# A linear-attention and gated-MLP kernel on one core: chunks 10 to 13 in the paired token layout, SBUF products on GpSimd alone from chunk 4 on, and another written-out order

## The chip, the core and the metric

The kernel runs on one of the eight cores of a Trainium2 chip. The core has a matrix engine (TensorE, PE in the profile), a vector engine (VectorE, DVE), an activation engine (ScalarE, ACT), a programmable engine (GpSimd, POOL) and a queue engine (SyncE, SP), which here does nothing but issue DMAs. Every engine takes its instructions strictly in the order in which they were written for it; between engines semaphores keep the order of data. The metric is the device time of one execution in microseconds (us). Three runs of the kernel before took 197.98, 200.19 and 202.25 us, median 200.19 us.

## The reference

There are 4 batches, 8 heads, 768 tokens and 48 numbers per head. The attention keeps a 48 x 48 state per head that is decayed and added to at each token; its output (3072 tokens by 384) goes through a two-layer MLP whose gate is `h * cos(h)`:

```python
f = 1.0 / (1.0 + np.exp(-f_logit))
for t in range(S):
    state = f[:, :, t, :, None] * state + np.einsum('bhd,bhe->bhde', k[:, :, t], v[:, :, t])
    y[:, :, t] = np.einsum('bhd,bhde->bhe', q[:, :, t], state)
# x = y as 3072 x 384
h = x @ w_in              # 384 -> 2048
out = (h * np.cos(h)) @ w_out   # 2048 -> 384
```

## The kernel before

**Tiling.** The 3072 tokens are 24 chunks of 128 tokens. Two chunks make a pair `n` (0 to 11), and three pairs a batch. Attention works pair by pair; the MLP works in units of `m`: units 0 and 1 are the two chunks of pair 0, and unit `m` from 2 on is pair `m - 1`.

**Attention of a pair**, by the names of its steps (`n.u` is the pair and which half of it; the uncut steps have no half):

- `f`, `k`, `q`, `v`: loads from HBM, issued on SP.
- `ex`, `ln` (ACT): log of the forget gate; `cum` (PE): running sums within a chunk; `eb`, `ei` (ACT): the decays `b` and `bi`.
- `qm` and `km`: the products q times b and k times bi, both factors in SBUF, result in bf16 in tile `qk`. `vb`: the cast of v to bf16. These may run on GpSimd or VectorE (`vb` on ScalarE too).
- `tq` (and `tk`): the transpose of the products into `qkt`. For pairs 0 to 3 it is done by PE into PSUM and copied out (`qkt`); for pairs 4 to 11 it is one DMA transpose per half, issued on SP.
- `sc` (PE): scores; `am` (DVE): mask, PSUM to SBUF. `ps` (PE), `st` (DVE) and `sz` (two instructions, r = 0 and 1): the new state and its decay. `sz` from tile `st` has both factors in SBUF and may run on GpSimd or VectorE.
- `y` and `yi` (PE): the output, from the scores and from the old state. `yb` (ACT or DVE): its cast. `tx`: its transpose into `x`, for pairs 4 to 10 one DMA transpose per half on SP, otherwise PE and a copy `xe`.

**MLP of a unit**: `h` (PE, eight steps), `co` (ACT, cosine), `g` (DVE, h times cosine, from PSUM and SBUF), `o` (PE, four steps per chunk), `ot` (copy) and `out` (store, on SP). `w` loads the weights and `wc` casts them.

**Two layouts.** In the paired layout (function `pair`) a partition holds two consecutive tokens, so that a run in HBM is 384 bytes; the even and odd tokens are separate blocks on PE. In the other (function `orderly`) a partition holds one token, a run is 192 bytes, and each of `f`, `k`, `q`, `v` is two DMAs per pair instead of one. Which pairs are orderly is set by `ORDERLY`, in the kernel before pairs 5 to 11, which are chunks 10 to 23. `gate` writes `g` straight for orderly pairs (L673) and swaps even and odd tokens back for the others (L677).

**Order.** The text `ORDER` sets everything. A word such as `km4.1:V2` says: step `km4.1` next, on the engine of that letter (T PE, S ACT, V DVE, G POOL, Y SP), and with which buffer. Function `emit` walks the words and issues each step, so an engine's order is that of its words. There is no scheduler behind it. `zf` steps are matmuls on zeros, whose results nobody reads.

Names that differ only in a number are buffers of a small pool: `qk` has 3 buffers, `x` 4, `yb` 4, `g` 5; the four PSUM tiles of 1024 columns are shared by all.

Of the kernel before, what the change touches and what calls it, by code (L numbers as in the profile page):

```python
# [183 lines left out]
def describe(nc, cpool, ppool, q, k, v, f_logit, moe_w_in, moe_w_out, out):  # L184
    G = Graph()
# [5 lines left out]
    def copy(e, o, i):  # L191
        (nc.scalar.copy if e == "ACT" else eng(e).tensor_copy)(out=o, in_=i)  # L192
# [629 lines left out]
```

## Time and profile before

| what | value |
|---|---|
| three runs | 197.98, 200.19, 202.25 us |
| profiled execution, its own time | 198.68 us |
| its span, first to last instruction | 196.9 us |
| busy: PE, DVE, ACT, POOL | 171.2, 145.2, 124.8, 58.1 us |
| mean granted TensorE clock | 0.991 |
| DMA queue q1 | 109024 packets, 35.47 MB, 79.4% of 16 engines' span |

The profile is one execution. Busy times are summed per engine; PE's overlapping matmuls make its share look fuller than it is. A row of the waits reads "who waited, for whom: us in total, times, longest". A row of the timeline reads "start, duration, engine, line, operation, result and operands, count", with the idle time of the engine ahead of it and what ended that in brackets. The rows of one tile give the shortest, median and longest duration in ns. SPq is the queue of DMA issues on SP.

### The profile page before, as it was taken

The page shows a single profiled execution, that of the slowest core. Times are in us where ns is not written, and L with a number is a line of the kernel's source. Part 1 is how long each engine was busy: PE and PEld are TensorE (multiplying, and loading weights), DVE is VectorE, ACT ScalarE, POOL GpSimd, SP SyncE. Part 2 cuts the span into 40 slices and gives each one's busy share as a digit, 9 for nine tenths or more (in the row PEclk, how much of TensorE's full clock was granted, in tenths as well). Part 3 has the DMA queues.
Part 4 walks back from the last instruction along what each step waited for, and adds up shares of the span by engine and source line. Part 5 has one row for each costly group of instructions (what it writes and reads, how often), then busy time and mean ns, then how long its engine had stood idle before and what let it go on. Part 6 is the DMA issues. An engine that isn't in the chain of part 4 may idle for free.

```text
span 196.9 us, 4992 instructions
## 1 busy us (share of the span) xinstructions
PE 171.2 (87%) x2077; PEld 126.2 (64%) x2077; DVE 145.2 (74%) x196; ACT 124.8 (63%) x149; POOL 58.1 (30%) x72
## 2 busy tenths in 40 slices
PE   7438879997999799798787998897989999999993
PEld 3227659966768556586576855674658866778651
DVE  6087988988799997588737894497689998667431
ACT  4936987996778767577456869596458730257401
POOL 3092489657009113511030201650251242000000
PEclk9997999999999999999999999999999999999999
DMA  6999999999995788798977999799949926402013
GB/s 148 272 262 309 379 290 320 228 338 265 188 251 127 83 172 174 179 199 156 210 142 152 226 192 180 165 172 223 198 108 188 191 46 139 150 3 83 0 40 122
DMA packets 109047, 35.79 MB, mean 182 GB/s; under 512 B 102368, under 2 KB 107488, under 8 KB 109024
## 3 DMA queue, kind: packets, MB, share of 16 engines
q1 hardware_dynamic: 109024, 35.47, 79.4%
q8 instruction: 16, 0.26, 0.6%
q14 instruction: 7, 0.06, 0.1%
HBM read 25.17 MB, written 4.72 MB: 152 GB/s over the span
## 4 chain that ended last, share of the span: by engine, by line
PE 48%; DMA 13%; DVE 6%; SPq 4%; ACT 2%; issue 2%; POOL 1%; DVEq 0%; POOLq 0%; ACTq 0%
PE ps L695 22%; PE ps L711 19%; DMA x<-yb 5%; DMA v<-in_v_dram 4%; DMA qkt<-qk 4%; DVE am L416 2%; SPq L385 2%; SPq L311 1%; PE ps L413 1%; PE ps L464 1%; DVE g L677 1%; PE ps L581 1%; PE ps L426 1%; PE ps L458 1%; DVE st L437 1%
## 5 line engine op out<-in xcount | busy, mean ns | idle before, releaser
L695 PE MATMUL ps<-x,w_in_bf 128*128 128x256 bf16 (+1 forms) x624 | 67.1, 264 | 9.6 <-DMA x<-yb 6.3
L711 PE MATMUL ps<-w_out_bf,g 128*128 128x384 bf16 x384 | 71.3, 326 | 0.0
L700 ACT ACTIVATE co<-ps,halfpi 128x1024 bf16<-128x1024 f32 x48 | 52.6, 1113 | 27.0 <-PE ps L695 26.8
L695 PEld LDWEIGHTS <-w_in_bf 128*128 128x128 bf16 x624 | 56.2, 98 | 18.4 <-issue 7.2
L711 PEld LDWEIGHTS <-g 128*128 128x128 bf16 x384 | 34.8, 98 | 19.3
L673 DVE TENSOR_TENSOR g<-ps,co 128x1024 bf16<-128x1024 f32 x28 | 33.6, 1220 | 9.2 <-ACT co L700 8.6
L677 DVE TENSOR_TENSOR g<-ps,co 128x1024 bf16<-128x1024 f32 x20 | 25.2, 1308 | 3.8 <-ACT co L700 2.7
L372 POOL TENSOR_TENSOR qk<-k,bi 128x384 bf16<-128x384 f32 x9 | 9.5, 1064 | 32.8 <-ACT bi L362 16.8
L416 DVE TENSOR_TENSOR am<-ps,upper 128x1024 bf16<-128x1024 f32 x14 | 16.7, 1220 | 2.5 <-PE ps L413 2.2
L192 ACT COPY ot<-ps 128x384 f32<-128x384 f32 x12 | 5.6, 479 | 12.2 <-PE ps L711 12.2
L192 DVE COPY ot<-ps 128x384 f32<-128x384 f32 x12 | 6.6, 551 | 9.1 <-PE ps L711 9.1
L533 POOL TENSOR_TENSOR qk<-q,b 128x384 bf16<-128x384 f32 x7 | 7.4, 1061 | 17.2 <-ACT b L524 10.0
L585 DVE TENSOR_TENSOR am<-ps,pmask 128x1024 bf16<-128x1024 f32 x10 | 12.0, 1215 | 0.6 <-PE ps L581 0.6
L372 POOL TENSOR_TENSOR qk<-q,b 128x384 bf16<-128x384 f32 x8 | 8.3, 1047 | 13.0 <-ACT b L362 11.2
L192 ACT CAST yb<-ps 128x384 bf16<-128x384 f32 x11 | 5.3, 479 | 10.4 <-PE ps L458 8.8
L533 DVE TENSOR_TENSOR qk<-k,bi 128x384 bf16<-128x384 f32 x5 | 7.6, 1539 | 4.9 <-ACT bi L520 4.8
L192 POOL CAST vb<-v 128x768 bf16<-128x768 f32 x7 | 6.4, 915 | 15.2 <-DMA v<-in_v_dram 15.2
L626 POOL TENSOR_TENSOR sz<-st,b 64x192 bf16<-64x192 f32 x9 | 4.8, 528 | 18.5 <-DVE st L619 18.3
L750 ACT ACT_TABLE_LOAD x7 | 9.0, 1283 | 0.8 <-PEq L806 0.7
L192 DVE CAST yb<-ps 128x384 bf16<-128x384 f32 x13 | 7.0, 548 | 3.3 <-PE ps L464 1.8
L700 ACT ACT_TABLE_LOAD x7 | 9.0, 1283 | 0.5 <-DVE x L192 0.4
L362 ACT ACTIVATE bi<-ps 128x768 f32<-128x768 f32 x7 | 5.7, 812 | 4.5 <-PE ps L356 4.1
(87 smaller groups left out, 210.9 us busy)
## 6 DMA issues: line engine op xcount, KB each, us to landing
out_dram<-ot SPq DMA_DIRECT2D x24, 192.0 KB, 2.2
f<-in_f_logit_dram SPq DMA_DIRECT2D x18, 192.0 KB, 3.5
q<-in_q_dram SPq DMA_DIRECT2D x18, 192.0 KB, 4.1
k<-in_k_dram SPq DMA_DIRECT2D x18, 192.0 KB, 4.3
g<-in_moe_w_in_dram SPq DMA_DIRECT2D x4, 768.0 KB, 8.5
g<-in_moe_w_out_dram SPq DMA_DIRECT2D x4, 768.0 KB, 7.6
v<-in_v_dram SPq DMA_DIRECT2D x14, 192.0 KB, 3.5
v<-in_v_dram SPq DMA_DIRECT2D x5, 384.0 KB, 6.1
```

Of the source, the lines that this page charges most:

```text
L192: (nc.scalar.copy if e == "ACT" else eng(e).tensor_copy)(out=o, in_=i)
L362: G.step(f"{nm}{n}", ("ACT",), lambda e, dst=dst, sc=sc, w=w: nc.scalar.activation(out=dst.ap, in_=pc.ap.rearrange("p (g n) -> p g n", g=2 ...
L372: G.step(f"{nm}{n}.{g}", ("POOL", "DVE"), lambda e, g=g, j=j, src=src, dec=dec: eng(e).tensor_mul(out=qkp[g][j].ap[:, :, 0:D], in0=src.ap, ...
L416: G.step(f"am{n}.{g}", ("DVE",), lambda e, g=g, sc=sc: nc.vector.tensor_mul(out=am[g].ap.rearrange("p r b n -> p (r b) n"), in0=sc.ap.rear ...
L533: G.step(f"{nm}{n}.{u}", ("POOL", "DVE"), lambda e, u=u, j=j, src=src, dec=dec: eng(e).tensor_mul(out=qkp[u][j].ap[:, :, :, 0:D], in0=swap ...
L585: G.step(f"am{n}.{u}", ("DVE",), lambda e, u=u, sc=sc: nc.vector.tensor_mul(out=am[u].ap.rearrange("p r b n -> p (r b n)").rearrange("p (y ...
L673: nc.vector.tensor_mul(out=gv.ap, in0=ph.ap.rearrange("p (f n) -> p f n", n=T), in1=co.ap.rearrange("p (f n) -> p f n", n=T))
L677: nc.vector.tensor_mul(out=o.rearrange("p b (n e) -> p b e n", e=2), in0=ph.ap.rearrange("p (b e n) -> p b e n", e=2, n=64), in1=co.ap.rea ...
L695: nc.tensor.matmul(ph.ap[:, i * T:(i + 1) * T].rearrange("p (g t) -> p g t", t=C), lhsT=w_in_bf[:, kk, f0:f0 + 128], rhs=xa[:, :, kk, :], ...
L700: G.step(f"co{m}.{j}", ("ACT",), lambda e, ph=ph, co=co: nc.scalar.activation(out=co.ap, in_=ph.ap, func=AF.Sin, bias=halfpi), reads=[ph], ...
L711: nc.tensor.matmul(po.ap[:, 0:DM], lhsT=gT.ap[:, j, i * C:(i + 1) * C], rhs=w_out_bf[:, j, :], start=(po.first and j == 4 * s), stop=(po.f ...
L750: nc.scalar.preload_act_table_set("natural_log_exp_and_others")
```

## The change

Five things are edited, and `ORDER` is replaced as a whole:

1. `ORDERLY` is pairs 7 to 11 instead of 5 to 11: chunks 10 to 13 go to the paired layout, one DMA per pair and tensor, and their gate to the swapping form.
2. From pair 2 on (chunk 4), `qm`, `km` and the `sz` that read `st` may run on GpSimd alone, `vb` on GpSimd or ScalarE.
3. The casts of weights (`wc`) may run on GpSimd or ScalarE.
4. One matmul on zeros less (`ZEROS`, 14 instead of 15).
5. The new `ORDER` names other engines and another succession for nearly all steps. By engine it has `km` and `qm` 44 times on POOL and 4 times on DVE (before 29 and 19), `sz` 30 times on POOL and 10 on DVE (before 16 and 24), `vb` 7 times on POOL and 5 on ACT (before 7 POOL, 3 DVE, 2 ACT). SP issues 136 DMAs instead of 144; DVE executes 146 steps instead of 177.

```diff
-ORDERLY = range(5, 12)
+ORDERLY = range(7, 12)
-ZEROS = 15
+ZEROS = 14
 ORDER = """
-zf0:T0 zf1:T1 zf2:T2 zf3:T3 zf4:T4 zf5:T5 zf6:T6 zf7:T7 zqk.2:V zsp.1:G zf8:T6 f0.0:Y0 f1.0:Y1
...
+zf0:T0 zf1:T1 zf2:T2 zf3:T3 zf4:T4 zf5:T5 zf6:T6 zf7:T7 zsz.3:V zf8:T6 zsp.0:G f1.1:Y0 ex1.1:S
...
-        G.step(f"wc{part}.{i}", ("POOL", "DVE", "ACT"), lambda e: copy(e, dst.ap, view()),
+        G.step(f"wc{part}.{i}", ("POOL", "ACT"), lambda e: copy(e, dst.ap, view()),
...
-                G.step(f"{nm}{n}.{u}", ("POOL", "DVE"), lambda e, u=u, j=j, src=src, dec=dec: eng(e).tensor_mul(
+                G.step(f"{nm}{n}.{u}", ("POOL", "DVE") if cut else ("POOL",), lambda e, u=u, j=j, src=src, dec=dec: eng(e).tensor_mul(
...
-            G.step(f"vb{n}{u}", ("POOL", "DVE", "ACT"), lambda e, s=s, t=t: copy(e, flat(t.ap), flat(s.ap)),
+            G.step(f"vb{n}{u}", ("POOL", "DVE", "ACT") if cut else ("POOL", "ACT"), lambda e, s=s, t=t: copy(e, flat(t.ap), flat(s.ap)),
...
-                src, ap, who = st, (lambda st=st: st.ap), ("POOL", "DVE")
+                src, ap, who = st, (lambda st=st: st.ap), ("POOL", "DVE") if cut else ("POOL",)
```

The same edits stand in `orderly`, without the `if cut`, since no orderly pair is cut (pairs 0 and 1 are the cut ones: their loads come in halves).

Three places show the new order. The first is DVE and GpSimd around the products of pairs 4 and 5. `qk_2` holds the products of pair 4; its rows are the four of L533 (before) or L532 (after). `am` rows are masks, `g` gates, `x` copies of the transposed output of pair 3. DVE before:

```order
L192 COPY x_3_147<-ps_2_165 128x384
L192 COPY x_3_147<-ps_1_164 128x384
L192 COPY ot_2_159<-ps_2_165 128x384
L533 TENSOR_TENSOR qk_2_121<-k_2_103,bi_2_118 128x8x48 x2
L677 TENSOR_TENSOR g_4_152<-ps_3_166,co_3_156 128x8x2x64
L677 TENSOR_TENSOR g_0_148<-ps_0_163,co_0_153 128x8x2x64
L677 TENSOR_TENSOR g_0_148<-ps_2_165,co_1_154 128x8x2x64
```

DVE after, at the same place (one copy of `x` has gone to ACT):

```order
L191 CAST yb_3_143<-ps_2_165 128x384
L191 COPY x_3_147<-ps_3_166 128x384
L618 TENSOR_TENSOR st_0_138<-ps_0_163,sz_2_136 128x384
L676 TENSOR_TENSOR g_2_150<-ps_1_164,co_3_156 128x8x2x64
L676 TENSOR_TENSOR g_3_151<-ps_2_165,co_0_153 128x8x2x64
L676 TENSOR_TENSOR g_3_151<-ps_0_163,co_1_154 128x8x2x64
L676 TENSOR_TENSOR g_3_151<-ps_3_166,co_2_155 128x8x2x64
```

GpSimd after, the eight products of pairs 4 (`qk_2`) and 5 (`qk_0`) in one file:

```order
L191 CAST vb_1_123<-v_1_108 128x768
L532 TENSOR_TENSOR qk_2_121<-q_2_106,b_2_115 128x8x48
L532 TENSOR_TENSOR qk_2_121<-k_1_102,bi_2_118 128x8x48
L532 TENSOR_TENSOR qk_2_121<-q_2_106,b_2_115 128x8x48
L532 TENSOR_TENSOR qk_2_121<-k_1_102,bi_2_118 128x8x48
L532 TENSOR_TENSOR qk_0_119<-q_1_105,b_0_113 128x8x48
L532 TENSOR_TENSOR qk_0_119<-k_2_103,bi_1_117 128x8x48
L625 TENSOR_TENSOR sz_3_137<-st_0_138,b_1_114 64x4x48
L532 TENSOR_TENSOR qk_0_119<-k_2_103,bi_1_117 128x8x48
```

The two products that stood between the copies and the first gate on DVE stand on GpSimd now, in one row with six others.

The second place is SP around the output transposes of pair 4 (`x_1`), before:

```order
L335 DMA q_1_105<-in_q_dram 128x8x48 x2
L311 DMA_TRANSPOSE x_1_145<-yb_0_140 128x3x128
L718 DMA out_0_dram<-ot_3_160 128x384
L311 DMA_TRANSPOSE x_1_145<-yb_1_141 128x3x128
L335 DMA v_2_109<-in_v_dram 128x8x48
```

and after:

```order
L334 DMA q_0_104<-in_q_dram 128x8x48
L310 DMA_TRANSPOSE x_1_145<-yb_1_141 128x3x128
L310 DMA_TRANSPOSE x_1_145<-yb_0_140 128x3x128
L717 DMA out_0_dram<-ot_3_160 128x384
L290 DMA q_2_106<-in_q_dram 128x8x96
```

The store that stood between the two transposes stands behind them.

The third is SP around the output transposes of pair 5 (`x_0`), before:

```order
L718 DMA out_0_dram<-ot_1_158 128x384
L311 DMA_TRANSPOSE x_0_144<-yb_3_143 128x3x128
L335 DMA q_1_105<-in_q_dram 128x8x48
L335 DMA k_2_103<-in_k_dram 128x8x48
L311 DMA_TRANSPOSE x_0_144<-yb_2_142 128x3x128
```

and after, with the output transposes of pair 6 (`x_2`) at the end:

```order
L310 DMA_TRANSPOSE x_0_144<-yb_3_143 128x3x128
L310 DMA_TRANSPOSE x_0_144<-yb_2_142 128x3x128
L717 DMA out_0_dram<-ot_1_158 128x384
L334 DMA k_2_103<-in_k_dram 128x8x48
L334 DMA q_0_104<-in_q_dram 128x8x48
L334 DMA k_0_101<-in_k_dram 128x8x48
L334 DMA q_1_105<-in_q_dram 128x8x48
L310 DMA_TRANSPOSE x_2_146<-yb_1_141 128x3x128
L310 DMA_TRANSPOSE x_2_146<-yb_0_140 128x3x128
```

The two loads between the transposes of pair 5 have moved, and the transposes of pair 6 stand together behind four loads.

More of the change, by code (lines that the diff above doesn't have):

```diff
@@ new lines @@
+o13.1:T o13.0:T ot13:S2 tq9.0:Y1 sc8.0:T4 am8.0:V1 qm8.1:G f10.0:Y v9.0:Y o11.3:T1 km8.1:G
+cum11.0:T2 tq8.1:Y3 g8.3:V km9.1:G o15.2:T0 tq9.1:Y2 cum11.1:T ei11:S2 sz7.10:G ps8.0:T4 q11.1:Y
+y8.0:T5 o11.0:T eb11:S2 qm11.0:G0 yi8.0:T ex10:S ln10:S0 st8.0:V1 sz8.01:G1 sz8.00:G o11.1:T
+yb8.0:V1 tx8.0:Y1 sc8.1:T6 sc9.0:T2 sc9.1:T4 am8.1:V2 q10.0:Y2 o15.0:T o15.1:T y8.1:T6 yi8.1:T
+yb8.1:S0 out10:Y o11.2:T am9.1:V3 cum10.1:T4 v10.1:Y1 tx8.1:Y vb9:S0 cum10.0:T out5:Y eb10:S1
+o14.3:T7 am9.0:V0 ps9.0:T6 qm10.0:G1 sz9.01:V0 sz9.00:V k11.0:Y2 y9.0:T2 ps9.1:T3 out13:Y ei10:S0
@@ new lines @@
+co10.2:S3 sz9.11:G o16.0:T o12.1:T sc11.0:T2 sc10.0:T4 g10.2:V o17.2:T0 ps10.0:T1 am11.0:V1
+am10.0:V2 st10.0:V1 tq11.1:Y3 o12.2:T o16.3:T ot16:S0 v11.0:Y vb11:S1 sz10.00:G2 sz10.01:G ot12:S3
+sc10.1:T2 sc11.1:T4 am10.1:V0 yi10.0:T1 o17.1:T o19.0:T7 ps10.1:T2 yi10.1:T3 am11.1:V3 y10.1:T
+y10.0:T yb10.1:V1 yb10.0:V0 o18.2:T6 o19.3:T o18.0:T tx10.1:Y2 ps11.0:T3 o17.0:T o17.3:T y11.0:T1
+ot17:S2 y11.1:T4 tx10.0:Y o18.3:T st10.1:V0 sz10.11:G1 sz10.10:G yi11.0:T st11.0:V1 h11.31:T2
+sz11.01:G0 sz11.00:G h11.30:T yb11.0:V3 co11.3:S1 out12:Y yi11.1:T yb11.1:V2 o18.1:T h11.00:T0
@@ new lines @@
+tx11.1:T5 xe11.1:S3 tx11.0:T4 ot18:V3 o19.1:T xe11.0:V h12.30:T4 h12.31:T co12.3:S2 h11.01:T o19.2:T
+g11.3:V4 co11.0:S0 out16:Y h12.10:T2 h12.11:T co12.1:S3 out17:Y ot19:S0 out19:Y g12.3:V3 g11.0:V
+h11.20:T4 h11.21:T h11.10:T0 g12.1:V h12.20:T6 o20.3:T2 co11.2:S1 g11.2:V o21.0:T3 h11.11:T
+co11.1:S2 o22.1:T4 o21.2:T out18:Y g11.1:V o20.0:T o20.2:T h12.01:T0 h12.00:T co12.0:S0 o23.1:T5
+o22.3:T h12.21:T o23.3:T co12.2:S3 g12.0:V o22.0:T o23.0:T g12.2:V out15:Y o21.3:T o22.2:T ot22:S2
+o23.2:T out22:Y ot23:S0 out23:Y o21.1:T ot21:S3 out21:Y o20.1:T ot20:S1 out20:Y
@@ L371, in orderly @@
             for j, (nm, src, dec) in enumerate((("qm", qh[g], bt), ("km", kh[g], bi))):
-                G.step(f"{nm}{n}.{g}", ("POOL", "DVE"), lambda e, g=g, j=j, src=src, dec=dec: eng(e).tensor_mul(
+                G.step(f"{nm}{n}.{g}", ("POOL",), lambda e, g=g, j=j, src=src, dec=dec: eng(e).tensor_mul(
                     out=qkp[g][j].ap[:, :, 0:D], in0=src.ap,
@@ L376, in orderly @@
         vb = Val(vbS)
-        G.step(f"vb{n}", ("POOL", "DVE", "ACT"), lambda e: copy(e, flat(vb.ap), flat(vv.ap)),
+        G.step(f"vb{n}", ("POOL", "ACT"), lambda e: copy(e, flat(vb.ap), flat(vv.ap)),
                reads=[vv], writes=[vb])
@@ L438, in orderly @@
                     out=st.ap, in0=view(), in1=S0.ap), reads=[ps[g], S0], writes=[st])
-                src, ap, who = st, (lambda st=st: st.ap), ("POOL", "DVE")
+                src, ap, who = st, (lambda st=st: st.ap), ("POOL",)
             for r in range(2):
@@ L620, in pair @@
                     out=st.ap, in0=view(), in1=S0.ap), reads=[ps[g], S0], writes=[st])
-                src, ap, who = st, (lambda st=st: st.ap), ("POOL", "DVE")
+                src, ap, who = st, (lambda st=st: st.ap), ("POOL", "DVE") if cut else ("POOL",)
             for r in range(2):
```

129 lines of the change are left out of this document (55 added, 74 removed).

## The prediction

> **What bounds the kernel now.** I read the page first, then busy times by stage, then PE's waits, then the timeline at the longest of these. The page's first row and one stage (columns from the third on: PE, PE weight loads, DVE, ACT, POOL busy us, granted clock, DMA share, GB/s):
>
> ```profile
> PE 171.2 (87%) x2077; PEld 126.2 (64%) x2077; DVE 145.2 (74%) x196; ACT 124.8 (63%) x149; POOL 58.1 (30%) x72
> 26.70:47.10 20.40, 18.53 (x294) 15.70 (x294) 18.50 (x21) 17.10 (x18) 14.07 (x15) 1.00 1.06 289
> ```
>
> PE is the bound, but not a full one: 196.9 less 171.2 leaves it idle for 25.7 us. DVE is next, and in the stage shown it is busy for as long as PE. GpSimd has 70% of its time free. So time is to be had where PE stands still, and PE's waits say for whom (total us, times, longest):
>
> ```profile
> PE ps L695 <- DMA x<-yb: 6.3, 5, 1.8
> PE ps L561 <- DVE qk L533: 2.6, 2, 1.7
> PE ps L413 <- DMA qkt<-qk: 1.7, 3, 1.0
> PE ps L695 <- DVE g L677: 1.2, 1, 1.2
> PE ps L695 <- DVE x L192: 1.1, 1, 1.1
> ```
>
> The largest is the MLP's first layer waiting for the DMA transpose of the attention output. The two waits for DVE in L695 have one story. The timeline around them, DVE, POOL and PE:
>
> ```profile
> 44.73 1.80 DVE L533 TENSOR_TENSOR qk<-k,bi 128x384 bf16<-128x384 f32 x1
> 44.65 1.47 POOL L192 CAST w_out_bf<-g 128x1536 bf16<-128x1536 f32 x1 [0.65 <-DMA g<-in_moe_w_out_dram]
> 47.11 0.38 PE L695 MATMUL ps<-x,w_in_bf 128*128 128x256 bf16 x2 [1.14 <-DVE x L192]
> 61.51 3.91 DVE L533 TENSOR_TENSOR qk<-k,bi 128x384 bf16<-128x384 f32 x2
> 60.86 0.99 POOL L372 TENSOR_TENSOR qk<-k,bi 128x384 bf16<-128x384 f32 x1
> 63.55 0.99 POOL L372 TENSOR_TENSOR qk<-q,b 128x384 bf16<-128x384 f32 x1
> 65.35 2.47 DVE L677 TENSOR_TENSOR g<-ps,co 128x1024 bf16<-128x1024 f32 x2
> 66.69 0.49 PE L695 MATMUL ps<-x,w_in_bf 128*128 128x256 bf16 x3 [1.23 <-DVE g L677]
> ```
>
> A DVE product ends only when GpSimd's row of work ends: 44.65 + 1.47 = 46.12, product over at 46.53; GpSimd busy from 60.86 to 64.54, the pair of products over at 65.42. The gate behind it starts at 65.35, and PE, which needs the gate's PSUM tile, stands for 1.23 us. The price list, per instruction (ns, shortest/median/longest):
>
> ```profile
> L372 POOL TENSOR_TENSOR qk<-k,bi x9: 993/1001/1372, 60.9 to 159.8; 128x384 bf16<-128x384 f32 x9
> L533 DVE TENSOR_TENSOR qk<-k,bi x5: 543/1346/3447, 9.4 to 64.9; 128x384 bf16<-128x384 f32 x5
> L443 DVE TENSOR_TENSOR sz<-st,b x11: 341/352/357, 84.3 to 166.5; 64x192 bf16<-64x192 f32 x11
> L626 POOL TENSOR_TENSOR sz<-st,b x9: 503/507/703, 20.7 to 80.4; 64x192 bf16<-64x192 f32 x9
> ```
>
> **The change part by part**, against the profiled execution's own 198.68 us.
>
> *Products off DVE.* 15 `qm` and `km` and 14 `sz` leave DVE, one weight cast and three `vb` too. DVE is relieved of at least 15 x 0.54 + 14 x 0.35 = 13.0 us, and of the stretching on top. The gain on the path is only where PE waited for it: 1.23 + 1.14 = 2.4 us. What would be late next there, the copies and cosines on the engines beside it, the list above does not show, so part may come back: I take -2.4 (0 to -2.4). On GpSimd the same work is 15 x 1.00 + 14 x 0.51 + 1.5 = 23.6 us more, 58.1 becoming about 82, still under half the span. A GpSimd product takes 1.00 us where DVE alone needs 0.54, so each chain from decay to scores grows by up to 2 x 0.46 us per half. The Trainium skill, page "GPSIMD Engine Reference", section "Engine selection", says that two-input elementwise work belongs on VectorE, GpSimd being about twice as slow; the rows agree on the factor (1.00 against 0.54), but not where both engines run (1.35 median). The page "SBUF — State Buffer", section "Who interferes with whom", has the reason: a VectorE instruction with two SBUF inputs contends with a GpSimd one that reads SBUF, and the later one is blocked; the 3.91 us row agrees.
>
> What waits now behind GpSimd's file: the eight products of pairs 4 and 5 with an `sz` in one row, 8 x 1.00 + 0.51 = 8.5 us. On PE a step of either layer takes 0.65 us, as this row of the chain of waits has it:
>
> ```profile
> 59.24 0.65 PE ps L711 x4
> ```
>
> Ten steps of the first layer and four of the second stand there between the output of pair 3 and the scores of pair 5, 14 x 0.65 = 9.1 us. So the row of products is covered, with little to spare. In two places the new order puts a product that needs a late decay ahead of an `sz` that PE needs (pairs 7 and 8). I put +0.8 us for it all (0 to +3: three places at the longest wait for `qkt`, 1.0).
>
> *Output transposes.* The rows of SP and PE, and the time to landing of `x`:
>
> ```profile
> 77.80 0.58 SPq L718 DMA_DIRECT2D out_dram<-ot  x1
> 78.88 1.18 SPq L311 DMA_TRANSPOSE x<-yb  x1
> 81.27 0.50 PE L695 MATMUL ps<-x,w_in_bf 128*128 128x256 bf16 x3 [1.28 <-DMA x<-yb]
> 94.81 0.58 SPq L335 DMA_DIRECT2D q<-in_q_dram  x1
> 95.44 0.58 SPq L335 DMA_DIRECT2D k<-in_k_dram  x1
> 96.12 1.48 SPq L311 DMA_TRANSPOSE x<-yb  x1
> 99.13 0.81 PE L695 MATMUL ps<-x,w_in_bf 128*128 128x256 bf16 x6 [1.84 <-DMA x<-yb]
> 105.24 0.49 PE L695 MATMUL ps<-x,w_in_bf 128*128 128x256 bf16 x3 [1.37 <-DMA x<-yb]
> DMA to landing us min/median/max: 2.3/2.5/4.7
> ```
>
> For pair 4 the second transpose is queued behind a store; without it, its issue can start 0.58 to 1.08 us sooner (78.88 - 77.80), of a wait of 1.28. For pair 5 it is two loads, 0.58 + 0.58 + 0.1 = 1.26 of 1.84; besides, the new order puts 11 steps of the two layers between the output of pair 5 and its first layer, 7 us against a landing of 2.5. Pair 6 keeps its two transposes together, but its SP file is no longer right behind those of pair 5: I take 1.0 of 1.37. The other two waits make 6.3 - 4.5 = 1.8; half of it, 0.9. Sum -0.8 - 1.26 - 1.0 - 0.9 = -4.0 (0 to -6.3). What SP issues earlier here is free; the store that moves back, nobody waits for.
>
> *Score transposes.* PE's 1.7 us for `qkt`: in the new order those of pairs 4 and 5 are issued in one row, and 3 us or more of second-layer steps stand between the products and the scores of pairs 7 to 11. Taken: -1.2 (+1.7 to -1.7). All that stands behind the four in a row on SP (loads of pairs 6 to 9 and pair 4's output) waits with them; nothing of it is needed for some 5 us.
>
> *Layout of pairs 5 and 6.* Their running sums and outputs cost PE more. The chain of waits has both kinds, pair 4 and pair 9:
>
> ```profile
> 57.58 0.21 PE ps L505
> 57.78 0.08 PE ps L507
> 57.87 0.08 PE ps L508
> 57.95 0.08 PE ps L511 x4
> 73.28 0.29 PE ps L653 x8
> 74.32 0.51 PE ps L643 x32
> 116.96 0.16 PE ps L353
> 117.12 0.08 PE ps L356 x4
> 117.20 0.22 PE ps L458 x8
> 118.99 0.17 PE ps L464 x4
> ```
>
> Per pair: sums 2 x (0.45 - 0.24) = 0.42; outputs from scores 0.51 - 2 x 0.22 = 0.07; from state 2 x (0.29 - 0.17) = 0.24; scores and states, for which no rows are quoted, by the same proportion another 0.1 to 0.3. That is 0.8 to 1.0 per pair, +1.7 us for two, and PE being the bound, all of it counts. The DMA gain is half as many packets in these two pairs' loads; PE's list has no wait for a load after the start, so 0 on the path (a load late in GpSimd's file is a rival below). The swapping gate is 0.09 us longer on 8 gates of DVE, which has been relieved of 13: nothing.
>
> *Start.* PE's 2.6 us for L561 fall before the first layer starts. The new order starts with pair 1, still with four products on DVE, and casts all four first-layer weights on GpSimd in a row. With weights landing at the same time as before I see no side: 0 (-2.6 to +2.6). The matmul on zeros less, 0.2 us, ran in idle time.
>
> Sum: -2.4 + 0.8 - 4.0 - 1.2 + 1.7 + 0 = -5.1, so 198.68 - 5.1 = 193.6 us on the profile's footing. That execution was 0.75% under the median of the runs (200.19); on the median's footing it is 195.1. I take the middle, 194.3.
>
> **The rivals.** *Waits only move.* PE is given its tiles earlier by DVE, but the landing of transposes on a busy DMA (up to 4.7 us) sets the pace as before, and only -2.4 + 1.7 and a bit of the x term (-0.8) are left: 198.68 - 1.5 = 197.2, on the median 198.7. For it: five waits of like size on a queue, in an order that was written for this kernel as well; against it: two of them have a store or loads visibly in front. Chance 0.27.
>
> *GpSimd comes late and makes it slower.* Engines take work in order, so one late operand holds the file:
>
> ```profile
> POOL qk L372 <- DMA k<-in_k_dram: 15.9, 3, 9.2
> ```
>
> Before, such a stop hurt little, since DVE had half of the products. Now all products of the pair behind, and SP's transposes with everything queued after them, stop too. The point from which it decides is a hold of about 3 us, the spare at the scores. A stop of 9.2 us would cost about 6; with all three stops of that row at their mean (15.9 / 3 = 5.3) and one at its longest, 2 x 2.3 + 6.2 = 10.8 us, 198.68 - 5.1 + 10.8 = 204.4, on the median 206. Against it: two of the pairs concerned now need half as many issues on SP, and the list above has 16 us of stops on GpSimd at no cost that PE shows. Chance 0.11.
>
> *Each product's longer time is on the path.* 15 x 0.46 = 6.9 us, 198.68 - 5.1 + 6.9 = 200.5 us, on the median 202. The waits of PE above do not bear it out: the one for a product on DVE (L561) is in the start, where four products stay on DVE. Chance 0.03. It is the Trainium skill's rule named above ("GPSIMD Engine Reference", "Engine selection") that would make it so.
>
> **How the numbers follow.** Forecast 0.59, the rivals 0.27, 0.11 and 0.03. A measurement of this kernel can tell about 2%, so faster is under 196.2 us and slower over 204.2. The forecast is faster; the first and third rival, 198.7 and 202, are within 2%; the second is slower: 0.59, 0.30, 0.11. The forecast's own range is 188.5 (all of the x term's 6.3, half of the start's 2.6 and the GpSimd term gone: 5.1 + 2.3 + 1.3 + 0.8 = 9.5 off 198.68 is 189.2, rounded down to leave a little) to 197. The whole range goes up to 201, over the first rival with 2 us of spread. Left out are about 0.05 below, 0.11 of the second rival and 0.03 of the third.
>
> **What would show it.** In the changed kernel: no DVE product over 0.6 us after 27 us, and no first-layer wait for a gate around 66 us (products off DVE); waits for x<-yb under 2.5 us in total (output transposes); waits for qkt<-qk at 0.5 or less; POOL busy near 82 and DVE near 125 us; PE's L505 to L511 rows twice more. New waits of PE on POOL's `sz` or for `qkt`, each over 2 us, would be the second rival. If the first layer starts much later than 26.7 us, the start was mis-sized.

## The result and the profile after

The changed kernel takes 190.0 us (median of four runs, 188.57 to 193.11), the kernel before beside it 199.47 us: ratio 0.952, 95% interval 0.940 to 0.965, so 4.8% faster. Two later sets, on two chips, gave 0.955 (0.947 to 0.963) and 0.950 (0.943 to 0.957). The ratios leave out runs that a second, slower state of the core made longer, so they can differ from the quotient of the medians. The profiled execution took 190.66 us with a span of 188.9; before it was 198.68 and 196.9. The granted clock was 0.991 in both, so the two traces can be set side by side. Line numbers after are one lower than before's; in the experiments they are up to three lower still.

Busy times of the kernel after, then PE's list of waits (who waited, for whom: us in total, times, longest):

```profile
PE 172.0 (91%) x2194; PEld 126.7 (67%) x2196; DVE 122.9 (65%) x165; ACT 124.4 (66%) x149; POOL 78.9 (42%) x103
```

```profile
PE ps L694 <- DMA x<-yb: 2.7, 2, 1.4
PE ps L560 <- POOL qk L532: 1.7, 2, 0.9
PE ps L580 <- DMA qkt<-qk: 1.7, 2, 1.3
...
PE ps L412 <- DMA qkt<-qk: 1.2, 3, 0.4
...
PE ps L652 <- POOL sz L625: 0.9, 1, 0.9
```

PE is busy for as long as before (171.2). It stands idle for 188.9 - 172.0 = 16.9 us instead of 25.7. That is the whole gain, 8.8 less of idleness and 0.8 more of work. The output transposes cost 2.7 instead of 6.3, no first-layer step waits for a gate or for a copy on DVE, and the score transposes cost 2.9 (1.7 + 1.2) instead of 1.7. The waits for GpSimd (1.7 and 0.9) lie in the start.

The products, from the rows of tile `qk` (ns shortest/median/longest, then first and last start in us):

```profile
L532 DVE TENSOR_TENSOR qk<-k,bi x2: 544/551/558, 9.5 to 13.6; 128x384 bf16<-128x384 f32 x2
L532 DVE TENSOR_TENSOR qk<-q,b x2: 546/626/705, 12.5 to 13.1; 128x384 bf16<-128x384 f32 x2
L532 POOL TENSOR_TENSOR qk<-k,bi x12: 996/1002/1010, 7.3 to 82.3; 128x384 bf16<-128x384 f32 x12
L371 POOL TENSOR_TENSOR qk<-k,bi x10: 993/1000/1006, 93.1 to 144.1; 128x384 bf16<-128x384 f32 x10
```

DVE has four products, none starting after 13.6 us and none over 0.71 us, where before they went up to 3.45. GpSimd's take 1.00 us each, as before.

Where the time came from, by the start of the first-layer step that comes first in a unit: unit 3 at 43.22 (before 47.11), unit 5 at 77.41 (81.27), unit 7 at 98.12 (105.24), unit 9 at 133.51 (147.35), last unit 165.72 (175.77). These leads do not measure the gain one by one: the new order also brings first-layer steps forward past other work of PE, so that the 13.8 and 10.1 us at the last two are more than the 8.0 us by which the whole span is shorter. About 3 us come from the start, since the first layer begins sooner by that much:

```profile
26.70 1.47 PE L695 MATMUL ps<-x,w_in_bf 128*128 128x256 bf16 x12 [0.79 <-ACT x L192]
```

```profile
23.59 1.51 PE L694 MATMUL ps<-x,w_in_bf 128*128 128x128 bf16 x24 [0.17 <-ACT x L191]
```

The first row is before, the second after. The two steps are not the same one: before begins with unit 2, the new order with unit 0. At unit 3 the lead is 3.9 us, of which 1.1 are before's wait for a copy on DVE. The rest comes stop by stop after that. The one long stop that the new order adds stands at the scores of pair 4:

```profile
63.84 1.46 PE L710 MATMUL ps<-w_out_bf,g 128*128 128x384 bf16 x8
66.62 0.42 PE L580 MATMUL ps<-qkt 48*64 48x128 bf16 x16 [1.32 <-DMA qkt<-qk]
```

Its chain begins at SP, where k of pair 4 is issued late (first row), and goes on on GpSimd, which holds two of the eight products in a row for q and k:

```profile
51.46 1.27 SPq L290 DMA_DIRECT2D k<-in_k_dram  x1
```

```profile
56.18 1.00 POOL L532 TENSOR_TENSOR qk<-q,b 128x384 bf16<-128x384 f32 x1 [3.35 <-DMA q<-in_q_dram]
59.20 1.00 POOL L532 TENSOR_TENSOR qk<-k,bi 128x384 bf16<-128x384 f32 x1 [2.02 <-DMA k<-in_k_dram]
```

### The profile page after: what moved, and what is told of

The parts are those of the page before. It is cut to its first block, busy times and chain, and to the rows that moved or that the text cites. A ratio compares the mean times of both kernels' runs of the same rounds, so it can differ in the third digit from the quotient of the medians.

```text
span 188.9 us, 5223 instructions
## 1 busy us (share of the span) xinstructions
PE 172.0 (91%) x2194; PEld 126.7 (67%) x2196; DVE 122.9 (65%) x165; ACT 124.4 (66%) x149; POOL 78.9 (42%) x103
## 4 chain that ended last, share of the span: by engine, by line
PE 35%; DMA 32%; POOL 8%; SPq 8%; DVE 6%; ACT 5%; issue 3%; DVEq 0%; POOLq 0%
PE ps L710 17%; PE ps L694 12%; DMA qkt<-qk 7%; DMA k<-in_k_dram 6%; DMA g<-in_moe_w_in_dram 6%; DMA x<-yb 6%; POOL qk L532 4%; DVE g L676 4%; DMA q<-in_q_dram 4%; DMA f<-in_f_logit_dram 4%; ACT co L699 2%; SPq L290 2%; POOL qk L371 2%; SPq L334 2%; SPq L276 2%
## 5 line engine op out<-in xcount | busy, mean ns | idle before, releaser
L710 PE MATMUL ps<-w_out_bf,g 128*128 128x384 bf16 x384 | 70.4, 326 | 0.1
L672 DVE TENSOR_TENSOR g<-ps,co 128x1024 bf16<-128x1024 f32 x20 | 24.1, 1221 | 17.9 <-ACT co L699 17.8
L584 DVE TENSOR_TENSOR am<-ps,pmask 128x1024 bf16<-128x1024 f32 x14 | 16.9, 1216 | 4.0 <-PE ps L580 4.0
L371 POOL TENSOR_TENSOR qk<-q,b 128x384 bf16<-128x384 f32 x10 | 9.9, 1000 | 14.4 <-ACT b L361 7.9
L625 POOL TENSOR_TENSOR sz<-st,b 64x192 bf16<-64x192 f32 x16 | 8.1, 506 | 18.2 <-DVE st L618 17.7
L532 POOL TENSOR_TENSOR qk<-k,bi 128x384 bf16<-128x384 f32 x12 | 12.0, 1002 | 7.9 <-ACT bi L519 4.7
L532 POOL TENSOR_TENSOR qk<-q,b 128x384 bf16<-128x384 f32 x12 | 12.1, 1016 | 6.4 <-DMA q<-in_q_dram 6.2
L191 DVE CAST yb<-ps 128x384 bf16<-128x384 f32 x16 | 8.7, 552 | 9.3 <-PE ps L463 4.3
L371 POOL TENSOR_TENSOR qk<-k,bi 128x384 bf16<-128x384 f32 x10 | 9.9, 1000 | 8.2 <-DMA k<-in_k_dram 5.7
L415 DVE TENSOR_TENSOR am<-ps,upper 128x1024 bf16<-128x1024 f32 x10 | 11.8, 1216 | 1.4 <-PE ps L412 1.4
L442 POOL TENSOR_TENSOR sz<-st,b 64x192 bf16<-64x192 f32 x14 | 7.0, 503 | 10.6 <-DVE st L436 10.0
L191 ACT CAST yb<-ps 128x384 bf16<-128x384 f32 x8 | 3.8, 479 | 8.0 <-PE ps L642 4.5
L490 ACT ACTIVATE f<-f 128x768 f32<-128x768 f32 (+1 forms) x9 | 6.3, 697 | 4.2 <-DMA f<-in_f_logit_dram 4.2
```

The costliest lines, as they stand in the source:

```text
L371: G.step(f"{nm}{n}.{g}", ("POOL",), lambda e, g=g, j=j, src=src, dec=dec: eng(e).tensor_mul(out=qkp[g][j].ap[:, :, 0:D], in0=src.ap, in1=d ...
L415: G.step(f"am{n}.{g}", ("DVE",), lambda e, g=g, sc=sc: nc.vector.tensor_mul(out=am[g].ap.rearrange("p r b n -> p (r b) n"), in0=sc.ap.rear ...
L532: G.step(f"{nm}{n}.{u}", ("POOL", "DVE") if cut else ("POOL",), lambda e, u=u, j=j, src=src, dec=dec: eng(e).tensor_mul(out=qkp[u][j].ap[: ...
L584: G.step(f"am{n}.{u}", ("DVE",), lambda e, u=u, sc=sc: nc.vector.tensor_mul(out=am[u].ap.rearrange("p r b n -> p (r b n)").rearrange("p (y ...
L625: eng(e).tensor_mul(out=new.ap[s, :, r, :].rearrange("p (u a) n -> p u a n", u=2), in0=ap()[s, :, r, :].rearrange("p (u a) n -> p u a n", ...
L672: nc.vector.tensor_mul(out=gv.ap, in0=ph.ap.rearrange("p (f n) -> p f n", n=T), in1=co.ap.rearrange("p (f n) -> p f n", n=T))
```

## The experiments

The theory taken into the first set was the prediction's: products on DVE are stretched by GpSimd, and output transposes are late because of what SP has ahead of them. The rival was that the order alone does it.

### Products to GpSimd in the order of before

Of before's order, 32 words change their engine and nothing else: 15 products, 14 `sz` and three `vb`.

```diff
-... km4.1:V km4.0:V ... vb7:V1 ... sz6.10:V3 sz6.11:V ...
+... km4.1:G km4.0:G ... vb7:G1 ... sz6.10:G3 sz6.11:G ...
```

> The kernel before with its own order; only the 32 steps of pairs 2 to 11 that VectorE had (15 products, 14 state decays, three casts of v) stand on GpSimd, at the same place in the text. Theory (the products were costly on VectorE because GpSimd ran beside them): no VectorE product after 27 us over 0.6 us, VectorE busy near 123 us instead of 145, the two waits of PE near 46 and 65 us (1.14 and 1.23 us) are gone, the waits for x<-yb (6.3 us) stay, since nothing of SP is moved; 1 to 2.4 us faster than before, 197.1 to 198.5 against 199.5. Rival (GpSimd comes late in an order that was not written for it): PE's waits for qkt or sz grow by over 2 us, and the time is 201 or more. Second rival (the order does it all): within 0.5 us of before, no wait gone.

Measured: 197.57 us, median of ten runs, beside 197.89 for the kernel before (13 runs). That is no difference. The trace shows what was expected of DVE (busy 124.9) and of the waits, in that the gate and the copy no longer appear in PE's list for the first layer, save one of 0.6 for a copy on ACT in the start. The waits for the transposes stay:

```profile
PE ps L692 <- DMA x<-yb: 5.3, 6, 1.6
```

PE's idle time fell from 25.7 to 195.1 - 173.2 = 21.9 us and the span from 196.9 to 195.1. PE's busy time was 2.0 us longer in this trace, at a granted clock of 0.974 against 0.991. So the stops did go, but a time gain worth the name does not follow from the engine alone. That the transposes, 5.3 us of waits, still set the pace in before's order is argued from this list and not shown by a run. (The trace of before is from another set, so single differences of 1 to 2 us between the two traces carry little weight.)

### Products back to DVE in the new order

The changed kernel with its 32 words back on V (31 from GpSimd, one cast from ScalarE).

```diff
-... km3.1:G2 ... qm5.1:G0 vb5:G1 ... km4.1:G km4.0:G ...
+... km3.1:V2 ... qm5.1:V0 vb5:V1 ... km4.1:V km4.0:V ...
```

> The changed kernel with its own order; the same 32 steps go back from GpSimd to VectorE, at the same place in the text. Theory (two engines reading SBUF at once stretch each other): products on VectorE of 1 us and more come back, VectorE busy 140 us or more, PE waits again for g, x or yb of VectorE, and the time is 2 to 5 us over the changed kernel's 190.0, so 192 to 195. Rival (the order did it all, the engine of the products does not matter): 189 to 191.

Measured: 215.1 us, ratio to before 1.091 (1.084 to 1.098). That is 25 us over the changed kernel and far over what either theory allowed. DVE is busy for 140.0 us, less than in the kernel before (145.2). So stretching is not the reason. PE's longest stop in this trace, and what DVE does there:

```profile
47.17 0.82 PE L314 MATMUL ps<-ident,yb 128*128 128x128 bf16 x6 [4.79 <-DVE yb L188]
```

```profile
46.08 0.56 DVE L529 TENSOR_TENSOR qk<-k,bi 128x384 bf16<-128x384 f32 x1 [5.27 <-DMA k<-in_k_dram]
46.56 0.55 DVE L188 CAST yb<-ps 128x384 bf16<-128x384 f32 x1
```

One product waits for a load of k for 5.27 us at the head of DVE's file, and the cast of the attention output, for which PE waits, stands behind it. The next two long stops of PE, 3.53 us at 91.91 and 3.60 at 157.21, wait for a copy `ot` on DVE, each behind a product that waits for its load (5.13 and 4.63 us). Against the changed kernel PE is idle for 35.0 us instead of 16.9, and busy for 177.8 instead of 172.0; the second goes with a granted clock of 0.50 behind the long stops (last section). DVE's waits for loads in this kernel and in the kernel before:

```profile
DVE qk L529 <- DMA k<-in_k_dram: 10.8, 2, 5.5
DVE qk L529 <- DMA q<-in_q_dram: 6.3, 3, 5.1
...
DVE qk L368 <- DMA k<-in_k_dram: 4.6, 1, 4.6
...
DVE vb L188 <- DMA v<-in_v_dram: 2.7, 1, 2.7
```

```profile
DVE vb L192 <- DMA v<-in_v_dram: 3.3, 1, 3.3
DVE qk L372 <- DMA k<-in_k_dram: 2.3, 2, 2.1
DVE qk L533 <- DMA q<-in_q_dram: 0.4, 1, 0.4
```

That is 24.4 us here and 6.0 before. Without the start (5.5 of k here, 0.4 of q before) it is 18.9 and 5.6, and in the changed kernel none; its one wait for a load, 5.4 us, is that of the start. This is the second theory: what counts is less how long a product takes than whose file it holds while its operand is still landing. On DVE the casts, copies and gates that free PSUM tiles stand behind it; on GpSimd only other products do.

### Output transposes together in the order of before

Only SP's words move in the kernel before: in pairs 4, 5, 7, 8 and 9 what stood between or ahead of the two transposes stands behind them. In this kernel the store of chunk 14 reads a buffer that already holds the rows of chunk 11.

```diff
-tx4.0 out3 tx4.1 ... tx5.0 q7.0 k7.0 tx5.1 f8.1 v7.1 q7.1 tx6.0 tx6.1 ...
+tx4.0 tx4.1 out3 ... tx5.0 tx5.1 q7.0 k7.0 f8.1 v7.1 q7.1 tx6.0 tx6.1 ...
```

> The kernel before; only SP's order is changed: in pairs 4, 5, 7, 8 and 9 the store or the loads that stood between or ahead of the two output transposes stand behind them. Theory (the transposes were late because of what SP had ahead of them): PE's waits for x<-yb go from 6.3 to 2.5 to 3.5 us, 2 to 4 us faster than before, 195.5 to 197.5. Rival (waits only move: DMA landing times set the pace, or the loads moved back are late): x<-yb stays over 5 us or as much comes up in other waits, within 1 us of before's 199.5.

Measured: 202.04 us (four runs, 199.92 to 205.57) beside 197.89; the ratio, 1.013 (1.008 to 1.018), is that of the two shorter runs, and the trace that of the longest. The stop of pair 5's first layer (1.84 before) went under 0.5; that of pair 6 grew from 1.37 to 3.55, still for its transposes. The prediction's account by SP's issues alone falls in this order.

### The same with the loads of pair 7 pushed back as well

To see whether the stop had only met the next transpose, v and q of pair 7 were also put behind the transposes of pair 6.

```diff
-tx5.0 q7.0 k7.0 tx5.1 f8.1 v7.1 q7.1 tx6.0 tx6.1
+tx5.0 tx5.1 q7.0 k7.0 f8.1 tx6.0 tx6.1 v7.1 q7.1
```

> The kernel before; on SP the store and all loads that stood between or right ahead of the output transposes of pairs 4, 5 and 6 (store of chunk 3; q and k halves of pair 7; v and q halves of pair 7) stand behind them. In the earlier set only the first two places were cleared, and the stop went from the first layer of pair 5 to that of pair 6. Theory (issue time ahead of a transpose is on the path, and a load pushed back one place must not meet the next transpose): stops ahead of the first layers of pairs 4, 5 and 6 (1.4, 2.0, 1.5 us) shrink by 2.5 us or more in sum, time 1 to 1.5% under before. Rival (the loads pushed back are now late for the products of pair 7, or the stops move on to pairs 7 and 8): no gain, within 0.5% of before.

Measured: 198.86 beside 198.97 us, ratio 1.0005 (0.995 to 1.006): no gain, the rival. At pair 5's first layer the kernel is 2.7 us ahead of before (96.42 against 99.13), and the lead goes at the next stop. Pair 6's first layer, whose transposes now issue 2.5 us sooner (97.33 instead of 99.85), waits longer still, and for something else:

```profile
105.52 1.89 PE L692 MATMUL ps<-x,w_in_bf 128*128 128x256 bf16 x8 [4.35 <-DVE ot L189]
```

```profile
104.17 0.56 DVE L189 CAST vb<-v 128x768 bf16<-128x768 f32 x1 [6.59 <-DMA v<-in_v_dram]
104.65 0.34 DVE L440 TENSOR_TENSOR sz<-st,b 64x192 bf16<-64x192 f32 x1
104.92 0.54 DVE L189 COPY ot<-ps 128x384 f32<-128x384 f32 x1
```

The cast of v on DVE waits 6.59 us for the load that was pushed back, and the copy `ot`, which frees the PSUM tile, stands behind it. The same cast in the kernel before and in the kernel of the section above:

```profile
101.69 0.56 DVE L192 CAST vb<-v 128x768 bf16<-128x768 f32 x1 [3.34 <-DMA v<-in_v_dram]
```

```profile
103.17 1.12 DVE L189 CAST vb<-v 128x768 bf16<-128x768 f32 x1 [4.91 <-DMA v<-in_v_dram]
```

DVE is held for 3.34, 4.91 and 6.59 us, and the copy behind it ends at 102.97, 105.03 and 105.46 us. In before that is early enough: PE has first-layer steps until 103.87, and its stop of 1.37 is for the transposes. In the kernel of the section above PE stands from 101.85; the copy, if PE needs it there too, would have held it for 3.2 us, and the transposes did for 3.55. Here the copy is what ends the stop of 4.35. This bears the second theory out at one place: in before's order the load of v of pair 7 cannot be put behind the transposes of pair 6, because a file that PE needs is waiting for that load. The stop costs more than its length: behind it the granted clock falls to 0.50 (last section), and PE is busy for 20.2 us from 105.5 to 126.2, where before it does the same number of matmuls in 17.8.

### Transposes apart in the new order

```diff
-tx4.0 tx4.1 out3 ... tx5.0 tx5.1 out2 k7.0 q7.1
+tx4.0 out3 tx4.1 ... tx5.0 k7.0 q7.1 tx5.1 out2
```

> The changed kernel; only SP's order is changed: the store of chunk 3 stands between the two output transposes of pair 4 again, and two loads (half of k and of q of pair 7) between those of pair 5. Theory of the prediction (what SP has ahead of a transpose is on the path, 0.8 us and 1.26 us): PE's waits for x<-yb go up by 1 to 2 us, and the time by as much, 191 to 192 where the changed kernel has 190. Rival (these two places are covered by other steps of PE in the new order, so SP's order there decides nothing): no wait comes up, time within 0.5 us of the changed kernel.

Measured: 192.73 us, ratio to before 0.973 (0.966 to 0.980), beside 0.955 for the changed kernel in the same set. One new long stop, at pair 5, and one of 0.16 us at pair 4. PE, and SP around it:

```profile
92.99 1.46 PE L691 MATMUL ps<-x,w_in_bf 128*128 128x256 bf16 x6 [3.17 <-DMA x<-yb]
```

```profile
86.87 1.87 SPq L331 DMA_DIRECT2D k<-in_k_dram  x1
88.79 0.57 SPq L331 DMA_DIRECT2D q<-in_q_dram  x1
89.41 1.68 SPq L307 DMA_TRANSPOSE x<-yb  x1
```

The second transpose issues at 89.41 instead of about 86.8 in the unchanged kernel of this set, 2.6 us later; PE's last unit ends 2.5 us later. The two are not one and the same. PE's waits for transposes grow only from 3.7 to 4.4 us, since the stops of 0.53 and 1.63 at pairs 5 and 6 go as the new one comes. From 92.00 to 107.30, behind the new stop, the granted clock is 0.78, and PE is busy for 14.3 us where the unchanged kernel needs 11.7 for these steps. So much of the trace's lag is the lower clock that came with the stop. The time is longer in all four runs (191.51 to 193.66, against 188.02 to 190.82). So with the products off DVE the order of SP decides where other steps don't cover it, as the prediction had it for pair 5; the store at pair 4 was covered but for 0.16 us.

### Pairs 5 and 6 in the other layout

```diff
-ORDERLY = range(7, 12)
+ORDERLY = range(5, 12)
-... q5:Y1 v5:Y1 f6:Y0 v6:Y2 q4:Y2 k4:Y1 ...
+... q5.0:Y1 q5.1:Y v5.0:Y1 v5.1:Y f6.0:Y0 f6.1:Y v6.0:Y2 v6.1:Y q4:Y2 k4:Y1 ...
```

> The changed kernel with pairs 5 and 6 back in the layout of one token to a partition: their loads are 16 DMAs instead of 8, their sums and outputs on PE the cheaper forms, their gates unswapped; the order of all steps is the changed kernel's, the added loads behind their twins. Theory (the layout costs PE 1.7 us for these two pairs, and the loads are hidden): PE busy 1.5 to 2 us less, time 188.3, about 1.7 us under the changed kernel's 190.0. Rival (the doubled loads on a full SP queue between 24 and 56 us come late): the wait for the scores of pair 4 near 65 us (1.5 us) grows by 2 us or more, 191 to 194.

Measured: 193.13 us, ratio to before 0.976 (0.971 to 0.981; the trace is of the longest of four runs), where the changed kernel has 0.950 to 0.955. On PE the layout costs about what was estimated: 14 groups of attention matmuls sum to 50.6 us after and 49.1 here. But eight more issues stand on SP, q and k of pair 4 are issued at 53.29 and 54.38 instead of 50.10 and 51.46, and the stop that they lead to doubles:

```profile
68.33 0.42 PE L578 MATMUL ps<-qkt 48*64 48x128 bf16 x16 [2.70 <-DMA qkt<-qk]
```

By unit 8 this kernel is 1.9 us behind (117.16 against 115.26), although PE has less to do. The 2.5 us that it loses between units 8 and 9 go with a granted clock of 0.92 in that stage of this trace (last section), so the trace explains by loads only about half of the difference of the four runs.

### The start of before, under the new order

All attention steps of pairs 0 and 1 up to the first layer, on every engine, as before; the weights' loads and all the rest as after. SP's first words:

```diff
-f1.1 q1.1 f1.0 k1.1 f0.0 q1.0 f0.1 k1.0 ...
+f0.0 f1.0 f0.1 q1.0 f1.1 k0.1 k0.0 q0.1 ...
```

> The changed kernel, but all attention steps of pairs 0 and 1 up to the first step of the first layer, with what stands among them on every engine, in the order, on the engines and in the buffers of the kernel before; the loads of the first layer's weights stay in the changed kernel's order. Theory (the 3.1 us by which the first layer starts sooner come from this order and are kept to the end): first layer at 26 to 27 us instead of 23.6, time 2.5 to 3.5 us over the changed kernel. Rival (the start's gain is absorbed later, since loads and the DMA queue set the pace between 24 and 56 us): first layer at 26 to 27 us, PE's waits after it shorter by 2 us or more, time within 1 us of the changed kernel. Second rival (the start's gain has to do with the weights' order): first layer at 24 us.

Measured: 191.89 us, ratio to before 0.968 (0.962 to 0.974), beside 0.955 (0.947 to 0.963) in this set. The first layer starts at 26.85 us, in the unchanged kernel beside it at 23.13: the start's gain is in the order of this part. How much of it lasts is not settled. By the ratios it is 1.3%, 2.6 us; in the profiles the 3.7 us have shrunk to 1.6 at unit 5 and to 0.4 at the end of the last unit, in part since the stop at the scores of pair 4 is gone here (0.7 in the kernel beside it): its chain hangs on loads, which did not move. The profiles favour this kernel: its own is of the shortest of its four runs (191.24 us), that of the kernel beside it of the longest (190.82, of 188.02 to 190.82).

### All start products on DVE

```diff
-km0.0:V2 qm0.0:V qm1.0:V1 qm0.1:G km0.1:V km1.1:G km1.0:G qm1.1:G
+km0.0:V2 qm0.0:V qm1.0:V1 qm0.1:V km0.1:V km1.1:V km1.0:V qm1.1:V
```

> The kernel before; only the four start products that GpSimd had (pairs 0 and 1) stand on VectorE, so that all eight are there, at their places in the text. Theory (VectorE's start products are long, 0.55 to 1.35 us, because GpSimd multiplies beside them): all eight take 0.54 to 0.6 us on VectorE, the last one ends no later than before (14.8 us) although VectorE has twice as many, and the first step of the first layer comes no later than before's 26.7 us. Rival (their length comes from loads that land late or from the weights' traffic): products of 0.9 us and more stay, the last ends 2 us later, first layer at 28 us or more.

Measured (one run): 201.33 us, first layer at 27.63 us, in a trace with a low granted clock from 15 to 35 us. DVE's products, and GpSimd at the same time:

```profile
9.72 0.56 DVE L530 TENSOR_TENSOR qk<-k,bi 128x384 bf16<-128x384 f32 x1 [5.20 <-ACT bi L517]
...
12.78 1.49 DVE L530 TENSOR_TENSOR qk<-k,bi 128x384 bf16<-128x384 f32 x3
14.19 1.18 DVE L530 TENSOR_TENSOR qk<-q,b 128x384 bf16<-128x384 f32 x1
```

```profile
13.89 1.06 POOL L189 CAST vb<-v 128x768 bf16<-128x768 f32 x1 [11.36 <-DMA v<-in_v_dram]
```

Seven of the eight take 0.55 us. The eighth starts while GpSimd casts v, takes 1.18 and ends 0.42 us after the cast. So the stretching is what the prediction said it was. But the eight end at 15.37, no sooner than with four on each engine (14.80, from a start 0.36 us earlier): it is not why the start got shorter.

### Two attempts at a faster kernel

The changed kernel with q and k of pair 4 ahead of f and v of pair 6 on SP, and with 0.8 us of other work of PE ahead of the first layer of pair 10:

```diff
-... v5 f6 v6 q4 k4 ...        ... yi11.0 h11.31 h11.30 yi11.1 o18.1
+... v5 q4 k4 f6 v6 ...        ... yi11.0 yi11.1 o18.1 h11.31 h11.30
```

> The changed kernel with two moves: on SP the loads of q and k of pair 4 ahead of f and v of pair 6, and on PE one step of the second layer and half an output of pair 11 ahead of the first layer of pair 10. Theory (the stop of 1.48 us ahead of the scores of pair 4 comes from a late k, that of 1.57 us ahead of the first layer of pair 10 lacks 0.8 us of other work): the first goes to under 0.3 us, the second to under 0.9, 1.5 to 2 us under the changed kernel, ratio to it 0.99. Rival (waits only move: f and v of pair 6 are late now, or PE stops elsewhere for as long): same stops in sum, time within 0.5 us of the changed kernel.

Measured: 190.83 us beside 188.62, ratio to before 0.965 against 0.955. Both stops shrank as expected, the first under 0.3, the second from 1.57 to 0.34, and another of 1.59 came at 58 us: the logarithm's input f of pair 6 is late now, on ACT, and a cast that PE needs stands behind it.

```profile
55.62 0.85 ACT L487 ACTIVATE f<-f 128x768 f32<-128x768 f32 x1 [3.37 <-DMA f<-in_f_logit_dram]
56.50 0.84 ACT L490 ACTIVATE sp<-f 128x768 bf16<-128x768 f32 x1
57.25 0.46 ACT L188 COPY ot<-ps 128x384 f32<-128x384 f32 x1
57.60 0.48 ACT L188 CAST yb<-ps 128x384 bf16<-128x384 f32 x1
```

The two profiled executions took 190.47 us here and 190.82 for the kernel beside it, so the traces do not show where the 2.2 us between the medians lie.

The next one therefore left f where it was, moved v of pair 6 back, and two loads behind pair 6's transposes:

```diff
-... v5 f6 v6 q4 k4 ... k9.0 q8.0 tx6.0 tx6.1 f11.0 v7.1 v7.0 ...
+... v5 f6 q4 k4 v6 ... tx6.0 tx6.1 f11.0 v7.1 v7.0 k9.0 q8.0 ...
```

> The changed kernel with three moves. SP: the load of v of pair 6 behind q and k of pair 4; two loads (k of pair 9, q of pair 8) from ahead of the output transposes of pair 6 to three places behind them. PE: one step of the second layer and half an output of pair 11 ahead of the first layer of pair 10. Theory: the stop ahead of the scores of pair 4 (0.9 to 1.5 us) shrinks by the 1.3 us of the one load moved back, that of pair 6's first layer (1.4 to 1.8) by 0.5 to 1.5 us as its transposes issue up to 0.3 us sooner behind a shorter queue, that of pair 10's (1.6 to 1.7) by 0.8: 2 to 3 us in all, 1 to 1.5% under the changed kernel beside it. Rival (waits only move, as with the two moves before): sum of the stops within 0.7 us, time within 0.5%.

> The changed kernel, unchanged, beside the three above on the same chip. Expected ratio to the kernel before 0.945 to 0.965; the kernel with three moves is compared with this one.

Measured: 189.49 us against 189.07 for the unchanged kernel beside it: no difference. The three stops, 0.51, 1.02 and 1.55 us in the kernel beside it, shrank to under 0.3, 0.36 and 0.43, and 1.30 us came up at the scores of pair 7, where none had been. No version beat the changed kernel. Its numbers in the set of the first attempt, 188.62 us:

> The changed kernel, unchanged, so that the kernels of this set have it beside them on the same chip. Expected: the ratio to the kernel before as measured, 0.94 to 0.965, and stops of PE of 1.2 us and more at the same three places: ahead of the scores of pair 4 near 65 us, of the first layer of pair 6 near 97 us and of pair 10 near 160 us.

It came out as expected but for the first stop, 0.7 us there.

## Why the prediction was right, and where it was not

It forecast faster, 194.3 us; the kernel is faster still, by 4.3 us, inside the range. That the number came so near is in part luck: the start's term was missed by 3.1 us and that of the score transposes by 2.4 the other way. Step by step:

- **Products off DVE (-2.4).** Size right: both waits for DVE are gone, 1.23 + 1.14 = 2.4 us. The reason was half of it. Stretching is real (the eighth product above), but the prediction read DVE's rows for durations alone and not for what DVE waited for, 6.0 us of loads. Alone, the edit gave 0.3 us that can't be told from nothing.
- **GpSimd's single file (+0.8).** After the start PE waits neither for `sz` nor for a product on GpSimd as such. "Covered, with little to spare" held for the length of the row; the row began late because q and k of pair 4 were late. That cost is in the next but one term. The second rival's mechanism (a late operand holds the row) did occur, with holds of 3.35 and 2.02 us, and cost 1.3, not 6.
- **Output transposes (-4.0).** Measured -3.6; the waits come to 2.7 us, where "under 2.5" was to show it. What the term lacked is a condition: in before's order like moves on SP gave +1.3% and nothing. In the second of these DVE's file, waiting for the load that was pushed back, is what held PE; in the first it was the transposes of the next pair. The first rival, "waits only move", is right for that order and for both attempts at a faster kernel, and wrong for the whole change.
- **Score transposes (-1.2).** The wrong sign: +1.2, from 1.7 to 2.9, where 0.5 or less was to show it. Where PE waited before, at pairs 7 to 11, it waits for 1.2 instead of 1.7 us, the right way and too little. The step that failed is the row of pairs 4 and 5: it was put at no cost, being covered by PE's steps, but it started late, and PE now waits for 1.7 us at scores where no DMA transpose had kept it waiting.
- **Layout of pairs 5 and 6 (+1.7).** PE's price is right (1.5). The failed step is "0 on the path" for the loads: undone, the time grows by 3 to 5 us (by the medians and by the ratios) instead of falling by 1.7. That no load stood in PE's list of waits did not mean that loads were not in the chains behind those waits; SP's issue times were not costed.
- **Start (0).** The largest miss, -3.1 in the profile. "I see no side" looked at products and weights, and not at what the first product waits for. In both kernels that is, last of all, the decay `bi` from ACT (first pair of rows before, second after):

```profile
8.84 0.48 ACT L520 ACTIVATE bi<-ps 128x384 f32<-128x384 f32 x1
9.36 0.56 DVE L533 TENSOR_TENSOR qk<-k,bi 128x384 bf16<-128x384 f32 x1 [4.82 <-ACT bi L520]
```

```profile
6.71 0.47 ACT L519 ACTIVATE bi<-ps 128x384 f32<-128x384 f32 x1
7.27 1.00 POOL L532 TENSOR_TENSOR qk<-k,bi 128x384 bf16<-128x384 f32 x1 [4.73 <-ACT bi L519]
```

  Before, ACT makes the logs of all four halves and two `b` ahead of the first `bi`; after, the logs of two halves. The first k is also issued 1.1 us sooner (fourth DMA instead of sixth, 2.33 instead of 3.43), and needs it: with 4.1 to 4.9 us from issue to landing, before's k came at about 8 us or later. Which of the two counts for how much of the 3.1 us, no run separated; the kernel with before's start, on ACT and SP alike, has its first layer at 26.85 us. How much of it reaches the end lies between 0.4 us, by profiles that favour the small figure, and 2.6 by the ratios.
- **"Each product's longer time is on the path."** No: 1.00 us each, and faster. The Trainium skill's rule in "GPSIMD Engine Reference", "Engine selection", to put two-input elementwise work on VectorE, is right about the factor of two (1.00 against 0.55) but not in its conclusion for this kernel: the one that follows it for these 32 steps in the new order takes 215.1 us, 25 more. (That order was written for products on GpSimd; the kernel before, whose order has them on both engines, takes 199.47.)

The terms -2.4, -3.6, +1.2, +1.5 and -3.1 sum to -6.4, of -8.0 in the profiles. Of the missing 1.6 us, 1.3 are three small waits of before for DVE and GpSimd in the later pairs (0.6, 0.5 and 0.2 us, at L426 and L458) that the list after lacks; the rest was not traced. Undoing the start, SP's order or the layout alone costs about 2.6, 3.6 and 4 us, together more than the change gained, so the parts are not additive.

## What to carry to other kernels

Before moving an instruction to a faster engine, look at what it waits for: one that waits for a load belongs in the file behind which nothing stands that PE needs, even at twice its duration. Look at every engine's own waits for DMA, not only at PE's list, and cost each issue on the DMA queue, from the first one on. An order and an assignment of engines are worth testing crosswise (each alone): here the assignment alone changed nothing and the order without it made the kernel 9% slower. And read the granted clock behind a long stop of PE before putting a whole delay down to the stop.
